# Seven block products for the second token block's first weight set, four of its weight remainders on GpSimd after attention, and a re-ordered end of attention

## The chip, the cores and the metric

The kernel runs on one core of one Trainium2 chip. The metric is the device time of one execution in microseconds. The core's engines run side by side, each with its own queue: TensorE (PE, with PEld for loading weights), VectorE (DVE), ScalarE (ACT), GpSimd (POOL) and SyncE (SP), which issues most of the transfers.

## The reference

Attention with a position bias comes first, then a layer of three "experts" of which the largest is taken:

```python
scores = scale * np.matmul(q, k.transpose(0, 1, 3, 2))        # 4 batches, 8 heads, 576 x 576
h = np.maximum(x @ w1 + b1, 0.0); bias = h @ w2               # x: relative position, 32 hidden units
scores = scores + bias.transpose(2, 0, 1)[None, :, :, :]
attn = exp(scores - max); attn = attn / (sum(attn) + 1e-09)
attn_out = np.matmul(attn, v)                                  # head size 64
x = attn_out as 2304 tokens x 512
h = np.maximum(np.maximum(x @ moe_w1, x @ moe_w2), x @ moe_w3) # 512 x 768 each
out = h @ moe_w_out                                            # 768 x 512
```

Everything is float32. The kernel gets near that with TensorE's rounded 32-bit type by splitting each operand into a rounded "high" part and a "low" remainder, and multiplying high by high, low by high and high by low.

## The kernel before

**Stages.** The bias comes first (to about 84 us), with attention running behind it. Attention has 72 steps (8 pairs of heads by 9 query tiles) and four more, 72 to 75, in which it drains: `tp` and `lp` are transposes of the normalised probabilities `e`, ScalarE and VectorE copy them to `et`, and the products `pv` (and `pvlast`) with the values follow. `e` is normalised by GpSimd (L325). When a `pv` accumulator is full, VectorE copies it out into the raw token tiles, printed as `xb` (L413). The expert part begins at 263.2 us, and the output product follows it from about 450.

**Expert part.** Tokens lie in three blocks x = 0, 1, 2 of 768 (2 by `TW` = 384), the weights in nine sets of four 256-wide parts. A set times a block is a `group` of seven block products, as in Strassen's scheme: p1, p5, p6, p2, p7, p4, p3, of the weight parts and their sums and of the token parts b11, b12, b21, b22 and the sums t1 to t4. For set 0 and the blocks 1 and 2 it is `plain`: eight products without sums. A block product is six matmuls of 128x384 (L654 to L656: high by high, low by high, high by low, for two halves). In a group p1, p6, p7 and p4 add into one PSUM bank, and between them ScalarE copies that bank out:

```python
nc.scalar.copy(o["m1"], made("p1"))                 # printed as m, L688
nc.scalar.copy(o["u2"], made("p6", "p1"))           # printed as u, L696
arith(v, o["q"][:, 1], made("p2"), o["m1"], ALU.add)
nc.scalar.copy(u3, made("p7", "p1"))                # printed as u, L703
nc.scalar.copy(acc[:, 0], made("p4", "p1"))         # printed as ht, L710
```

`acc` and, in set 0, `q` are printed as `ht`. p5 has a bank of its own, to which p3 adds.

**Splitting.** For a token part `high` is a cast by ScalarE (L567, the names ending in h), `low` a subtraction with two inputs from SBUF (`arith`, L542, ending in l) on VectorE or GpSimd, `sum` an addition or subtraction by VectorE (printed as `t`). The sums build on each other: t1 = b12 - b11, t3 = b22 - b12, t2 = t3 + b11, t4 = b21 - t2; p5 uses t1, p6 the second sum t2, p7 t3, p4 the fourth sum t4. Block 0's tiles for these two are swapped by `home`: its second sum's parts are printed as `t4h` and `t4l`, its fourth sum's as `t2h` and `t2l`. The tile `t2h` takes the place of the raw b21, so its cast waits until `b21l` is formed, and `t2l` that of the raw b22. Weights go the same way: `wh` is ScalarE's cast, `wl` the remainder (`low0(k)` for part k of set 0, `lower_w` for the later ones), `ws` the weight sums by GpSimd, `wr0p` the raw set 0, `wr` the raw set 1.

**What sets the order.** Each engine works through its queue in the order in which the program writes it; nothing is scheduled by itself. During attention the extra work is in streams: `w0` converts and splits weights, `pend` holds weight sums and two remainders, `early_x` and `late_x` split token block 0. The main loop says in which step a stream may emit its next piece, and `rest` empties them after step 75. In the expert part one slot belongs to each block product: the table of `F(...)` jobs in `moe` says which token and weight work is emitted in which slot, ahead of that slot's product. In the list that orders the products, `plain(1)` gives one product into the first group (behind p7), and all of `plain(1)` and `plain(2)` follow it.

Of the kernel before, what the change touches and what calls it, by code (L numbers as in the profile page):

```python
# [9 lines left out]
F32 = mybir.dt.float32  # L10
# [9 lines left out]
def kernel(  # L20
# [12 lines left out]
    nc = tc.nc  # L33
# [514 lines left out]
    class Blocks:  # L548
# [8 lines left out]
        def home(self, n, k):  # L557
            if self.x == 0 and n in ("t2", "t4"):
                n = "t4" if n == "t2" else "t2"
            if n in F_OF:  # L560
                return self.fin.tile(SHAPE, F32R, tag=f"f{self.x}_{F_OF[n] + k}", bufs=1, name=f"{n}{'hl'[k]}_{self.x}")
            return self.xa.tile(SHAPE, F32R, tag=f"r{self.x}_{R_OF[n] + k}", bufs=1, name=f"{n}{'hl'[k]}_{self.x}")
# [79 lines left out]
    def moe(pool, wpool, x0, xa, xb, raw, sr):  # L642
# [113 lines left out]
        for k, what in enumerate((  # L756
                (F(b1.high, "b11", "b21"), F(b1.low, "b11")),
                (F(b1.low, "b21"), F(b1.high, "b12")),
                (F(b1.low, "b12"), F(b1.high, "b22")),
                (F(b1.low, "b22"), F(b2.high, "b11")),  # L760
                (F(b1.sum, "t1"), F(b2.high, "b21")),
                (F(b2.low, "b11"), F(b2.high, "b12")),
                (F(b1.high, "t1"), F(b2.low, "b21"), F(b2.high, "b22")),
                (F(b1.low, "t1"),),
                (F(b2.low, "b12"),),
                (F(b2.low, "b22"),),
                (F(b1.sum, "t3"),),
                (F(b1.sum, "t2"), F(b1.high, "t3")),
                (F(b1.low, "t3"),),
                (F(b1.sum, "t4"), F(b1.high, "t2")),  # L770
                (F(b1.low, "t2"), F(b1.high, "t4")),
                (F(b1.low, "t4"), F(raise_w, 1, 0)),
                (F(b2.sum, "t1"), F(raise_w, 1, 1)),
                (F(lower_w, 1, 0, v, 3), F(b2.high, "t1")),
                (F(lower_w, 1, 3, v, 4),),
                (F(b2.low, "t1"),),
                (F(b2.sum, "t3"),),
                (F(b2.sum, "t2"), F(b2.high, "t3")),
                (F(b2.low, "t3"),),
        )):  # L780
            at(*((0, k) if k < 7 else divmod(k + 1, 8)), *what)
# [305 lines left out]

        c1, c2 = plain(1), plain(2)
        g0 = list(group(0, 0))
        for k, f in enumerate(g0[:5] + c1[:1] + g0[5:] + c1[1:] + c2):  # L1090
            now[:] = (0, k) if k < 7 else divmod(k + 1, 8)
            slot()
            f()
        groups = [group(s, x) for s in range(1, NSET) for x in range(NX)] + [out_pair(m) for m in range(NP)]
        groups[0][0]()
        for n, (_, p5, p6, p2, p7, p4, p3) in enumerate(groups[:-2]):
# [11 lines left out]
    with tc.manual_schedule():  # L1108
# [44 lines left out]
        class Pieces:  # L1153
# [8 lines left out]
            def go(self, scalar):  # L1162
                if not scalar:
                    for f in self.todo[:self.count]:
                        self.todo.pop(0)()
# [7 lines left out]
        def first():  # L1173
# [8 lines left out]

            def sums(raw, name, k=None):
                got = {}

                def piece(n):
                    if n == 0:
                        got["sr"] = sum_tile(wpool, name)
                        got["gen"] = sum_w(raw, got["sr"])
                        next(got["gen"])  # L1190
# [41 lines left out]
            sums0, got = sums(raw0, "0")  # L1232
            pend.extend(sums0 + [lambda k=k: low0(k) for k in (2, 7)])
            yield "vector"
# [5 lines left out]
            nc.scalar.copy(hi[:, 768:1792], got["sr"])  # L1240
            for k in (3, 5):
                yield "vector"
                low0(k, nc.vector, 2)
            yield from conv(lambda: half(made1, 1, ()), "1_1")
            make, got1 = sums(made1[0], "1")
            pend.extend(make)
            last.update(raw=made1[0], got=got1)

# [16 lines left out]
        def late_x():  # L1265
            for j in range(2):
                yield "vector"
                x0.sum("t3", j)
            yield "vector"
            x0.sum("t2")  # L1270
            yield "scalar"
            x0.high("t3", "b21")
            yield "vector"
            x0.low("t3")
            yield "scalar"
            x0.high("t2")
            yield "vector"
            x0.sum("t4")
            x0.low("t2")
            yield "scalar"  # L1280
            x0.high("b22")
            yield "vector"
            x0.low("b21")
            x0.low("b22")

        ex, lx = Stream(early_x()), Stream(late_x())
        while n < NSTEP + LAG:
# [4 lines left out]
            if n % NS in (3, 5, 8) and not early and n < NSTEP - 3 or n in (NSTEP - 3, NSTEP - 2):  # L1292
                pend.count = 2 if n == 6 * NS - 1 else 1
                more += [pend]
            if early:
                more.insert(0, ex)
            if n >= NSTEP or n in (NSTEP - 3, NSTEP - 1):
                more.insert(0, lx)
# [4 lines left out]
        for w in (w0, pend, ex, lx):  # L1303
            w.rest()
        x0.high("t4")
        x0.low("t4")
        at.split_x()
        apool.release()
# [51 lines left out]
```

## Time and profile before

| what | value |
|---|---|
| median of 3 runs | 534.76 us (534.66 to 535.26) |
| profiled execution, time | 534.38 us |
| profiled execution, span of its instructions | 532.6 us |
| TensorE busy | 522.8 us, 98% of the span |
| VectorE busy | 438.3 us, 82% |
| ScalarE busy | 358.7 us, 67% |
| GpSimd busy | 263.7 us, 50% |
| TensorE's granted clock, mean | 1.000 |
| transfers | 78.66 MB, mean 148 GB/s |

The span runs from the first instruction to the last; 1.8 us of the execution lie around it. Busy is the time in which an engine has an instruction under way. Rows of the trace give start, length, engine, line and operation, the tile that is written, `<-` the tiles that are read, then shape and count; in brackets stands the idle time before, with `<-` what ended it.

### The profile page before, as it was taken

How to read it: one execution, taken by the hardware profiler on the slowest of the kernel's cores; microseconds unless marked ns; L12 is line 12 of the kernel's file. 1: busy time of each engine (PE TensorE's matmuls, PEld its weight loads, DVE VectorE, ACT ScalarE, POOL GpSimd, SP SyncE). 2: the span in 40 equal slices, each digit the busy share in tenths (PEclk: the TensorE clock that was granted, in tenths of full speed). 3: DMA queues.
4: the chain of work that ended last, by engine and by line, in shares of the span. 5: the costliest groups of instructions: out<-in, count | busy, mean ns of one | idle time of the engine just before them, and what ended most of it. 6: DMA issues, size and time to landing. Idle time of an engine off the chain costs nothing.

```text
span 532.6 us, 13672 instructions
## 1 busy us (share of the span) xinstructions
PE 522.8 (98%) x5185; PEld 436.5 (82%) x5185; DVE 438.3 (82%) x929; ACT 358.7 (67%) x805; POOL 263.7 (50%) x294
## 2 busy tenths in 40 slices
PE   8999899999999999999999999999999999999997
PEld 5455667676767676666699999999999999999997
DVE  7998879898989898989999988648887456898883
ACT  7998989998989999888767343443434325465552
POOL 0003878678878897877302563646566535300000
DMA  5896998533774193111301215442175340856642
GB/s 162 239 337 175 348 269 233 166 107 109 223 216 150 26 252 120 55 23 36 109 0 41 78 42 196 140 159 78 56 261 180 140 147 1 255 171 188 190 148 80
DMA packets 73458, 78.66 MB, mean 148 GB/s; under 512 B 23152, under 2 KB 54512, under 8 KB 73392
## 3 DMA queue, kind: packets, MB, share of 16 engines
q1 hardware_dynamic: 73248, 77.49, 46.8%
q8 instruction: 41, 0.67, 0.5%
q10 hardware_dynamic: 144, 0.29, 0.2%
q14 instruction: 25, 0.20, 0.1%
HBM read 49.56 MB, written 27.94 MB: 146 GB/s over the span
## 4 chain that ended last, share of the span: by engine, by line
PE 86%; DVE 5%; ACT 3%; issue 2%; POOL 2%; DMA 1%; DVEq 0%; POOLq 0%; ACTq 0%
PE pv L393 14%; PE p L656 11%; PE p L654 11%; PE p L655 11%; PE s L287 10%; PE tp L352 6%; PE p_o L1031 4%; PE p_o L1030 4%; PE p_o L1029 4%; DVE hid L113 4%; PE bp L135 3%; ACT e L311 2%; PE lp L352 2%; PE s L277 1%; POOL e L325 1%
## 5 line engine op out<-in xcount | busy, mean ns | idle before, releaser
L325 POOL TENSOR_SCALAR e<-e,rc 128x576 f32<-128x576 f32 x144 | 111.7, 792 | 30.6 <-DVE rc L321 26.2
L297 DVE CUSTOM_DVE_ANT_0 sn<-s,bias 128x576 f32<-128x576 f32 x144 | 103.1, 754 | 21.7 <-PE lp L352 10.9
L311 ACT ACTIVATE e<-sn,nm 128x576 f32<-128x576 f32 x144 | 111.3, 780 | 3.8 <-DVE nm L297 3.5
L393 PE MATMUL pv<-et,vt 128*64 128x320 f32 (+1 forms) x496 | 74.0, 419 | 0.6 <-PE lp L352 0.6
L352 PE MATMUL tp<-ident,e 64*128 64x64 f32 x1152 | 53.2, 224 | 0.5 <-ACT et L463 0.3
L467 DVE COPY et<-tp 128x512 f32<-128x512 f32 x72 | 49.3, 685 | 3.8 <-PE tp L352 3.7
L463 ACT COPY et<-tp 128x512 f32<-128x512 f32 x72 | 41.8, 580 | 14.2 <-PE lp L352 13.6
L542 POOL TENSOR_TENSOR wl<-wr,wh 128x256 fp32r<-128x256 f32 x21 | 21.3, 1040 | 59.5 <-ACT wh L744 59.5
L287 PE MATMUL s<-kh,qh 64*128 64x288 f32 x240 | 48.0, 342 | 1.1 <-DVE nm L297 1.0
L352 PEld LDWEIGHTS tp<-ident,e 64*128 64x128 f32 x1152 | 47.3, 139 | 0.8 <-ACT et L463 0.5
L287 PEld LDWEIGHTS s<-kh,qh 64*128 64x128 f32 x240 | 28.0, 184 | 21.4 <-DVE nm L297 8.5
L393 PEld LDWEIGHTS pv<-et,vt 128*64 128x64 f32 x496 | 30.4, 136 | 18.2 <-issue 1.6
L696 ACT COPY u<-p 128x384 f32<-128x384 f32 x25 | 12.0, 480 | 43.1 <-PE p L656 42.8
L287 PE MATMUL s<-kl,qh 64*128 64x288 f32 x240 | 40.9, 296 | 0.0
L135 PE MATMUL bp<-hid,w2s 128*32 128x79 f32 (+51 forms) x640 | 39.9, 390 | 0.9 <-DVE hid L113 0.7
L287 PE MATMUL s<-kh,ql 64*128 64x288 f32 x240 | 39.8, 291 | 0.0
L113 DVE TENSOR_SCALAR hid<-sm,bp 128x528 f32<-128x528 f32 (+17 forms) x108 | 39.1, 443 | 0.0
L135 PEld LDWEIGHTS bp<-hid,w2s 128*32 128x32 f32 x640 | 19.9, 110 | 21.1 <-issue 15.4
L703 ACT COPY u<-p 128x384 f32<-128x384 f32 x25 | 12.0, 479 | 36.5 <-PE p L656 36.4
L542 POOL TENSOR_TENSOR wl<-ws,wh 128x256 fp32r<-128x256 f32 x28 | 29.2, 1070 | 13.1 <-ACT wh L746 13.1
L352 PE MATMUL lp<-ident,e 64*128 64x64 f32 x144 | 33.3, 231 | 2.3 <-POOL e L325 1.5
L542 DVE TENSOR_TENSOR q<-p,u 128x384 f32<-128x384 f32 x36 | 19.9, 553 | 17.4 <-ACT u L703 15.1
(236 smaller groups left out, 1621.0 us busy)
## 6 DMA issues: line engine op xcount, KB each, us to landing
bias_d<-bs SPq DMA_DIRECT2D x36, 295.5 KB, 5.6
bias<-bias_d SPq DMA_DIRECT2D x16, 576.0 KB, 5.4
w<-in_moe_w_dram SPq DMA_DIRECT2D x36, 256.0 KB, 3.2
h_d<-ht SPq DMA_DIRECT2D x18, 384.0 KB, 3.2
hin<-h_d SPq DMA_DIRECT2D x16, 384.0 KB, 4.6
qr<-in_qd_dram SPq DMA_DIRECT2D x16, 288.0 KB, 4.4
kr<-in_kd_dram SPq DMA_DIRECT2D x16, 288.0 KB, 5.4
vt<-in_v_dram SPq DMA_DIRECT2D x32, 128.0 KB, 3.4
```

The source lines that it names most:

```text
L113: marks["hid"] = nc.vector.tensor_scalar(out=h[:, 0:n], in0=wl[:, 0:n], scalar1=k["bp"][:, m:m + 1], scalar2=0.0, op0=ALU.add, op1=ALU.max)
L135: nc.tensor.matmul(bp[32 * c:32 * c + 32, o:o + w], lhsT=w2s, rhs=src, start=True, stop=True)
L287: nc.tensor.matmul(ss[h][:, x, 0:HALF], lhsT=u[q][p, 128 * t:128 * t + 128], rhs=u[k][p, cols], start=(j == 0), stop=(j == len(terms) - 1))
L297: nc.vector.tensor_tensor_reduce(out=sn.rearrange("p (a b) -> p a b", a=2), in0=st["s"][h][:, :, 0:HALF], in1=bt.rearrange("p (a b) -> p a ...
L311: nc.scalar.activation(st["e"][:, S * h:S * h + S], sn, ACTF.Exp, scale=-1.0, bias=nm, accum_out=self.sm[:, x:x + 1])
L325: nc.gpsimd.tensor_scalar(out=e, in0=e, scalar1=self.rc[:, x:x + 1], scalar2=1.0, op0=ALU.mult, op1=ALU.mult)
L352: return nc.tensor.transpose(to, e2[p, k0:k0 + 128], ident[p, p])
L393: nc.tensor.matmul(pv[p], lhsT=w, rhs=x, start=(c == 0), stop=(c == NTQ))
L542: eng.tensor_tensor(out=out, in0=f(a), in1=f(b), op=op)
L654: nc.tensor.matmul(o, lhsT=hi[:, c], rhs=h[:, j], start=first and j == 0, stop=False, **on)
L655: nc.tensor.matmul(o, lhsT=hi[:, c], rhs=l[:, j], start=False, stop=False, **on)
L656: nc.tensor.matmul(o, lhsT=lo[:, c], rhs=h[:, j], start=False, stop=last and j == 1, **on)
```

## The change

It touches only set 0 of the weights, the end of attention and the first slots of the expert part.

- Token block 1 takes set 0 in a `group` of seven products, as block 0 does. The products of set 0 now run: block 0's group with one plain product of block 2 in it, the other seven plain ones of block 2, then block 1's group with the first product of set 1 in it. The table of jobs is re-ordered for that: block 2's splits come first, block 1's sums earlier.
- `home` swaps the tiles of block 1's second and fourth sum as well.
- `pend` no longer holds the remainders 2 and 7 of set 0, and emits one piece at a time. The stream `w0` leaves out the remainders 5 and 6; the remainder 3 comes behind the conversion of set 1's second half, on VectorE, one part wide.
- Set 1's weight sums get a tile of the weight fetches' kind (`w64`).
- `late_x` forms the remainders of block 0's b21 and b22 on GpSimd, with set 0's remainder 2 between and 5, 7, 6 behind. Block 0's last sum, its cast and the remainders around it move behind the drain's steps, and VectorE's remainder of t3 moves behind an accumulator's copies.

```diff
         def home(self, n, k):
-            if self.x == 0 and n in ("t2", "t4"):
+            if self.x < 2 and n in ("t2", "t4"):
...
-                (F(b1.high, "b11", "b21"), F(b1.low, "b11")),
...
+                (F(b2.high, "b11", "b21"), F(b2.low, "b11")),
...
+                (F(b1.low, "b11"), F(b1.sum, "t1"), F(b1.high, "t1")),
...
-        c1, c2 = plain(1), plain(2)
-        g0 = list(group(0, 0))
-        for k, f in enumerate(g0[:5] + c1[:1] + g0[5:] + c1[1:] + c2):
+        groups = [group(s, x) for s in range(1, NSET) for x in range(NX)] + [out_pair(m) for m in range(NP)]
+        c2, g0, g1 = plain(2), group(0, 0), group(0, 1)
+        for k, f in enumerate((*g0[:5], c2[0], *g0[5:], *c2[1:], *g1[:5], groups[0][0], *g1[5:])):
             now[:] = (0, k) if k < 7 else divmod(k + 1, 8)
             slot()
             f()
-        groups = [group(s, x) for s in range(1, NSET) for x in range(NX)] + [out_pair(m) for m in range(NP)]
-        groups[0][0]()
...
-                    for f in self.todo[:self.count]:
+                    for f in self.todo[:1]:
...
-                        got["sr"] = sum_tile(wpool, name)
+                        got["sr"] = wpool.tile([128, 1024], F32, tag=tag, bufs=2 if tag == "w64" else 1, name=f"ws{name}")
...
-            pend.extend(sums0 + [lambda k=k: low0(k) for k in (2, 7)])
+            pend.extend(sums0)
...
-            for k in (3, 5):
-                yield "vector"
-                low0(k, nc.vector, 2)
+            yield "vector"
             yield from conv(lambda: half(made1, 1, ()), "1_1")
-            make, got1 = sums(made1[0], "1")
+            make, got1 = sums(made1[0], "1", tag="w64")
             pend.extend(make)
-            last.update(raw=made1[0], got=got1)
+            last.update(raw=made1[0], got=got1, low=low0)
+            yield "vector"
+            low0(3, nc.vector, 2)
...
         def late_x():
-            for j in range(2):
-                yield "vector"
-                x0.sum("t3", j)
             yield "vector"
+            x0.sum("t3", 0)
+            yield "vector"
+            x0.sum("t3", 1)
+            x0.high("t3")
             x0.sum("t2")
             yield "scalar"
-            x0.high("t3", "b21")
+            x0.high("b21")
             yield "vector"
-            x0.low("t3")
+            x0.low("b21", nc.gpsimd)
             yield "scalar"
             x0.high("t2")
             yield "vector"
-            x0.sum("t4")
-            x0.low("t2")
+            x0.low("t3")
+            last["low"](2)
             yield "scalar"
             x0.high("b22")
             yield "vector"
-            x0.low("b21")
-            x0.low("b22")
+            x0.low("b22", nc.gpsimd)
+            for k in (5, 7, 6):
+                last["low"](k)
...
-                pend.count = 2 if n == 6 * NS - 1 else 1
...
-            if n >= NSTEP or n in (NSTEP - 3, NSTEP - 1):
+            if n >= NSTEP or n == NSTEP - 3:
                 more.insert(0, lx)
...
+        x0.low("t2")
+        x0.sum("t4")
         x0.high("t4")
+        at.split_x()
         x0.low("t4")
-        at.split_x()
```

The following excerpts are each engine's order, one row per instruction or run of like ones; the numbers behind the names tell tiles apart.

GpSimd's queue before, from attention's last but two groups of `e` to the first remainders of weight set 1 (`wl_5734`, which wait for casts in the expert part):

```order
L542 TENSOR_TENSOR ws_5092<-wr_4353 128x256
L325 TENSOR_SCALAR e_5088<-e_5088,rc_5219 128x576 x2
L325 TENSOR_SCALAR e_5151<-e_5151,rc_5219 128x576 x2
L325 TENSOR_SCALAR e_5214<-e_5214,rc_5312 128x576 x2
L325 TENSOR_SCALAR e_5270<-e_5270,rc_5312 128x576 x2
L542 TENSOR_TENSOR ws_5092<-wr_4353,ws_5092 128x256
L542 TENSOR_TENSOR wl_5734<-wr_5470,wh_5733 128x256 x3
L542 TENSOR_TENSOR wl_5734<-ws_5712,wh_5733 128x256 x4
```

And the same place after; `b21l` and `b22l` are block 0's, `wl_3333` the remainders of weight set 0:

```order
L325 TENSOR_SCALAR e_5086<-e_5086,rc_5216 128x576 x2
L325 TENSOR_SCALAR e_5148<-e_5148,rc_5216 128x576 x2
L325 TENSOR_SCALAR e_5211<-e_5211,rc_5308 128x576 x2
L325 TENSOR_SCALAR e_5267<-e_5267,rc_5308 128x576 x2
L542 TENSOR_TENSOR b21l_5350<-xb_0_1171,b21h_5317 128x768
L542 TENSOR_TENSOR wl_3333<-wr0p,wh_3332 128x256
L542 TENSOR_TENSOR b22l_5424<-xb_0_1172,b22h_5393 128x768
L542 TENSOR_TENSOR wl_3333<-ws_3400,wh_3332 128x256
L542 TENSOR_TENSOR wl_3333<-wr0p,wh_3332 128x256
L542 TENSOR_TENSOR wl_3333<-ws_3400,wh_3332 128x256
L542 TENSOR_TENSOR wl_5730<-wr_5471,wh_5729 128x256 x3
```

Six subtractions now stand behind the last `e` where one weight sum stood. Two are 768 wide, four 256 wide.

VectorE's queue before, in the drain: `et` are copies of transposes, `xb` the copies out of the accumulators `pv` and `pvlast`, `t_0_5316` block 0's second sum and `t_0_5393` its fourth:

```order
L542 TENSOR_TENSOR t3l_5353<-t_0_5155,t3h_5318 128x768
L413 COPY xb_1_1175<-pv_1_5304 128x192
L413 COPY xb_2_1179<-pv_1_5304 128x64 x2
L467 COPY et_0_5360<-tp_7_1_5363 128x8x64
L542 TENSOR_TENSOR t_0_5393<-xb_0_1171,t_0_5316 128x768
L542 TENSOR_TENSOR t4l_5395<-t_0_5316,t4h_5355 128x768
L467 COPY et_0_5360<-tp_8_1_5401 128x8x64
L542 TENSOR_TENSOR b21l_5428<-xb_0_1171,b21h_5320 128x768
L542 TENSOR_TENSOR b22l_5430<-xb_0_1172,b22h_5397 128x768
L413 COPY xb_1_1176<-pv_1_5385 128x192
L413 COPY xb_2_1180<-pv_1_5385 128x64 x2
L542 TENSOR_TENSOR t2l_5449<-t_0_5393,t2h_5447 128x768
```

And after, where the second sum is `t_0_5315` and the fourth `t_0_5446`; the last row is the first remainder of the expert part:

```order
L413 COPY xb_1_1175<-pv_1_5300 128x192
L413 COPY xb_2_1179<-pv_1_5300 128x64 x2
L467 COPY et_0_5357<-tp_7_1_5360 128x8x64
L542 TENSOR_TENSOR t3l_5390<-t_0_5152,t3h_5313 128x768
L467 COPY et_0_5357<-tp_8_1_5397 128x8x64
L413 COPY xb_1_1176<-pv_1_5382 128x192
L413 COPY xb_2_1180<-pv_1_5382 128x64 x2
L542 TENSOR_TENSOR t4l_5444<-t_0_5315,t4h_5352 128x768
L542 TENSOR_TENSOR t_0_5446<-xb_0_1171,t_0_5315 128x768
L413 COPY xb_2_1180<-pvlast 128x256
L542 TENSOR_TENSOR t2l_5451<-t_0_5446,t2h_5448 128x768
L542 TENSOR_TENSOR b11l_5469<-xb_2_1178,b11h_5465 128x768
```

The accumulator's copies (`pv_1_5300`) moved ahead of `t3l`; `b21l` and `b22l` left the queue; `t4l` and the fourth sum moved behind the copies of the next accumulator.

ScalarE's queue before, at the beginning of the expert part (`m` and `u` are the copies of the shared bank, `t2h_5447` the cast of block 0's fourth sum):

```order
L567 CAST t2h_5447<-t_0_5393 128x768
L567 CAST b11h_5464<-xb_1_1174 128x768
L567 CAST b21h_5466<-xb_1_1175 128x768
L688 COPY m_0_5472<-p_0_0_5473 128x384
L567 CAST b12h_5483<-xb_1_1173 128x768
L567 CAST b22h_5494<-xb_1_1176 128x768
L696 COPY u_0_5496<-p_0_0_5473 128x384
L567 CAST b11h_5506<-xb_2_1178 128x768
L567 CAST b21h_5518<-xb_2_1179 128x768
L703 COPY u_0_5520<-p_0_0_5473 128x384
L567 CAST b12h_5531<-xb_2_1177 128x768
L567 CAST t1h_5540<-t_1_5516 128x768
```

And after, where the fourth sum's cast is `t2h_5448`:

```order
L1222 CAST wh_3332<-wr0p 128x256
L567 CAST t2h_5448<-t_0_5446 128x768
L567 CAST b11h_5465<-xb_2_1178 128x768
L567 CAST b21h_5467<-xb_2_1179 128x768
L688 COPY m_0_5473<-p_0_0_5474 128x384
L567 CAST b12h_5484<-xb_2_1177 128x768
L567 CAST b22h_5495<-xb_2_1180 128x768
L696 COPY u_0_5497<-p_0_0_5474 128x384
L567 CAST b11h_5507<-xb_1_1174 128x768
L567 CAST t1h_5521<-t_1_5519 128x768
L703 COPY u_0_5523<-p_0_0_5474 128x384
L567 CAST t3h_5543<-t_1_5534 128x768
```

The casts ahead of `m` are as many as before, of block 2 instead of block 1; ahead of the second `u` now stands the cast of block 1's first sum, `t1h_5521`, which stood behind it.

## Rows read from the trace of the kernel before

**Rows 1.** The page's busy times: engine, us, share of the span, instructions.

```profile
PE 522.8 (98%) x5185; PEld 436.5 (82%) x5185; DVE 438.3 (82%) x929; ACT 358.7 (67%) x805; POOL 263.7 (50%) x294
```

**Rows 2.** Stretches: bounds, length, busy PE, PEld, DVE, ACT, POOL; granted clock, DMA share, GB/s.

```profile
205.00:226.00 21.00, 20.09 (x273) 13.64 (x271) 19.33 (x50) 19.41 (x52) 15.66 (x18) 1.00 0.20 53
...
250.00:263.20 13.20, 11.96 (x138) 7.11 (x136) 11.94 (x25) 10.13 (x23) 7.41 (x8) 1.00 0.37 121
263.20:289.50 26.30, 26.30 (x153) 26.30 (x152) 24.97 (x31) 18.43 (x30) 0.00 (x0) 1.00 0.07 21
```

**Rows 3.** Timeline of TensorE, 205 to 236: start, length, operation, idle before.

```profile
217.11 0.27 PE L352 MATMUL lp<-ident,e 64*128 64x64 f32 x1 [0.26 <-POOL e L325]
...
220.36 0.27 PE L352 MATMUL lp<-ident,e 64*128 64x64 f32 x1 [0.47 <-POOL e L325]
```

**Rows 4.** Timeline of GpSimd, 186 to 296.

```profile
194.62 1.84 POOL L542 TENSOR_TENSOR t1l<-t,t1h 128x768 fp32r<-128x768 f32 x1
...
211.60 0.74 POOL L542 TENSOR_TENSOR wl<-wr0p,wh 128x256 fp32r<-128x256 f32 x1 [2.13 <-ACT wh L1225]
...
215.58 1.47 POOL L325 TENSOR_SCALAR e<-e,rc 128x576 f32<-128x576 f32 x2
...
253.19 4.14 POOL L325 TENSOR_SCALAR e<-e,rc 128x576 f32<-128x576 f32 x4 [0.62 <-DVE rc L321]
257.30 0.73 POOL L542 TENSOR_TENSOR ws<-wr,ws 128x256 f32<-128x256 f32 x1
```

**Rows 5.** Timeline of TensorE, drain and beginning of the expert part, 250 to 300.

```profile
257.35 1.84 PE L393 MATMUL pv<-et,vt 128*64 128x320 f32 x12 [0.43 <-PE lp L352]
...
260.41 0.71 PE L393 MATMUL pv<-et,vl 128*64 128x320 f32 x4
...
265.39 0.33 PE L654 MATMUL p<-t4h,wh 128*128 128x384 f32 x1
...
269.55 0.34 PE L654 MATMUL p<-t2h,wh 128*128 128x384 f32 x1
...
288.30 0.34 PE L654 MATMUL p<-t1h,wh 128*128 128x384 f32 x1
```

**Rows 6.** Timeline of ScalarE, 250 to 275.

```profile
261.51 0.84 ACT L567 CAST t2h<-t 128x768 fp32r<-128x768 f32 x1 [0.84 <-DVE b21l L542]
262.25 0.83 ACT L567 CAST b11h<-xb 128x768 fp32r<-128x768 f32 x1
...
264.55 0.48 ACT L688 COPY m<-p 128x384 f32<-128x384 f32 x1 [0.73 <-PE p L656]
...
268.71 0.48 ACT L703 COPY u<-p 128x384 f32<-128x384 f32 x1
```

**Rows 7.** Timeline of VectorE, 250 to 275.

```profile
255.57 1.15 DVE L542 TENSOR_TENSOR t3l<-t,t3h 128x768 fp32r<-128x768 f32 x1
256.64 0.61 DVE L413 COPY xb<-pv 128x192 f32<-128x192 f32 x3
...
257.77 1.07 DVE L542 TENSOR_TENSOR t<-xb,t 128x768 f32<-128x768 f32 x1
...
267.67 0.56 DVE L542 TENSOR_TENSOR ht<-p,m 128x384 f32<-128x384 f32 x1
268.15 0.95 DVE L542 TENSOR_TENSOR t<-xb,xb 128x768 f32<-128x768 f32 x1
...
269.70 0.95 DVE L542 TENSOR_TENSOR b11l<-xb,b11h 128x768 fp32r<-128x768 f32 x1
270.56 0.95 DVE L542 TENSOR_TENSOR b21l<-xb,b21h 128x768 fp32r<-128x768 f32 x1
```

**Rows 8.** Timeline of VectorE and GpSimd, 445 to 461.

```profile
450.19 5.11 POOL L542 TENSOR_TENSOR wop<-wop,wohp 128x768 fp32r<-128x768 f32 x2
...
454.42 1.29 DVE L542 TENSOR_TENSOR Cl<-C,Ch 128x384 fp32r<-128x384 f32 x1
...
458.82 0.55 DVE L542 TENSOR_TENSOR Al<-hin,Ah 128x384 fp32r<-128x384 f32 x1
```

More of the change, by code (lines that the diff above doesn't have):

```diff
@@ L756, in moe @@
         for k, what in enumerate((
-                (F(b1.high, "b11", "b21"), F(b1.low, "b11")),
[L758 to L774, printed above, removed]
+                (F(b2.high, "b11", "b21"), F(b2.low, "b11")),
+                (F(b2.low, "b21"), F(b2.high, "b12")),
+                (F(b2.low, "b12"), F(b2.high, "b22")),
+                (F(b2.low, "b22"), F(b1.high, "b11")),
+                (F(b1.low, "b11"), F(b1.sum, "t1"), F(b1.high, "t1")),
+                (F(b1.low, "t1"), F(b1.sum, "t3")),
+                (F(b1.high, "t3"), F(b1.sum, "t2")),
+                (F(b1.low, "t3"), F(b1.high, "t2")),
+                (F(b1.low, "t2"), F(b1.high, "b21")),
+                (F(b1.sum, "t4"),),
+                (F(b1.low, "b21"), F(b1.high, "b22")),
+                (F(b1.low, "b22"), F(b1.high, "t4")),
+                (F(b1.low, "t4"),),
+                (F(raise_w, 1, 0),),
+                (F(raise_w, 1, 1),),
+                (F(lower_w, 1, 0, v, 3),),
                 (F(lower_w, 1, 3, v, 4),),
+                (F(b2.sum, "t1"), F(b2.high, "t1")),
                 (F(b2.low, "t1"),),
@@ L1181, in conv, with sums @@
                     yield token
-            def sums(raw, name, k=None):
+            def sums(raw, name, k=None, tag="ws"):
                 got = {}
```

## The prediction

> **What bounds the kernel now.** I read the busy times first: TensorE has work in 98% of the span, VectorE follows with 82% [rows 1]. So the span is TensorE's own work plus its few waits, and an edit counts only if it removes matmuls or moves a wait. The table by stretch says where waits are left [rows 2]: 0.9 us in the stretch from 205 to 226, 1.2 us in the drain of attention (250 to 263.2), none in the first 26 us of the expert part, where TensorE is busy 26.30 of 26.30 us. The granted clock is 1.00, the 2.4 GHz level, in all three. Then I read single instructions. In 205 to 226 two waits of 0.26 and 0.47 us are for GpSimd's `e` [rows 3], while GpSimd itself had stood 2.13 us in front of a weight remainder `wl` [rows 4]. In the drain the reader should see a wait of 0.43 us in front of `pv` at 257.35 [rows 5]: VectorE copies out the old accumulator (256.64) only after `t3l` [rows 7].
>
> At the start of the expert part TensorE never waits, but by little. p1, p6, p7 and p4 of a group add into one PSUM bank, and ScalarE copies that bank out between them (m, u, u): p6 may start when m is copied, p4 when the second u is. m is done at 265.03 and p6 starts at 265.39; the second u is done at 269.19 and p4 starts at 269.55 [rows 5, 6]. The margin is 0.36 us both times. Both copies stand in ScalarE's queue behind casts that wait for VectorE.
>
> **What the change removes.** The second token block takes seven block products instead of eight. Six matmuls go; a block product lasts 1.04 us (four from 265.39 to 269.55) [rows 5]. From p4 of the first group to the second product of weight set 1 there are 18 block products before (269.55 to 288.30, that is 18.75 us) and 17 after: **-1.04 us**, all on the path.
>
> The weight remainders 2 and 7 leave GpSimd's queue in the middle of attention, and with the one at 211.60 the 2.13 us of standing that kept the `e` behind it late [rows 4]. Both waits of [rows 3] should go: -0.73 us at most, 0 if a conversion step of VectorE that now falls there holds up the scores instead. I take **-0.6**, near the upper end, since the released `e` at 215.58 can move by more than both waits together. The conversion of set 1's second half moves one slot earlier and the sums of set 1 move among the `e`: nothing, since GpSimd stands idle there before each group of `e`; without that cover a sum costs 0.73. SP's queue keeps its order; one weight fetch now waits for VectorE to finish set 1's remainders, and it is used some ten block products later: nothing.
>
> Copying out the accumulator before `t3l` takes away the 0.43 us at 257.35. I count that as nothing too, because something else is late next.
>
> **What it adds, first place: the drain.** After its last `e` GpSimd now has b21l, weight remainder 2, b22l, and remainders 5, 7, 6; it had one piece of 0.73 us. A 768-wide remainder takes GpSimd 1.84 us, a 256-wide one 0.74 [rows 4]; on VectorE 768 wide takes 0.95 [rows 7]. What matters is what the two do to each other. A 128x384 remainder takes VectorE 0.55 us at 458.82 (`Al`), and 1.29 us at 454.42 (`Cl`), where GpSimd's two remainders run from 450.19 to 455.30; it ends 0.41 us behind them [rows 8]. It waited until GpSimd's instruction was over. GpSimd's two took 2.56 each instead of 1.84, so it waits as well. The Trainium skill has this as a rule (SBUF — State Buffer, section "Who interferes with whom"): a VectorE instruction with two SBUF inputs and a GpSimd instruction that reads SBUF exclude each other for a whole instruction. By that rule the sum is the one below, by a mere tax it would be the first rival's; `Cl` agrees with the rule.
>
> So from the end of the last `e` (253.19 + 4.14 = 257.33) [rows 4] the two engines take turns, the earlier asker first: b21l 1.84, t3l 0.95, remainder 2 0.74, b22l 1.84, t4l (the remainder of the second sum) 0.95, remainder 5 0.74, the fourth sum 0.95. That is 8.01 us, so the fourth sum is ready at 265.34. Check that t4l comes behind b22l: b22l begins at 260.86, and t4l stands behind the copies of the accumulator that ends at 261.12, or 0.4 to 0.6 us earlier with the wait at 257.35 gone [rows 5]; three copies take 0.61 (256.64) [rows 7]: it asks at about 261.1 at the earliest. In the kernel before the fourth sum was formed at 257.77 and nothing waited.
>
> ScalarE's queue is t2h (the cast of that fourth sum), two casts of the third token block, then m. Casts follow each other at 0.74 us, m takes 0.48 [rows 6]: 265.34 + 2.22 + 0.48 = 268.04, with 0.1 for the handover (estimated) p6 starts at **268.1 instead of 265.39**. Behind the waiting cast stand m, and behind m TensorE.
>
> **Second place: p4.** In the new order the second u stands behind t1h of the second token block; t1h waits for VectorE's sum t1, that sum for b11l, and b11l stands behind the addition that waits for p2. From the end of p2: addition 0.48, b11l 0.87, sum 0.95, cast 0.74, u 0.48, handover 0.1: 3.62 us [rows 6, 7]. TensorE has only two block products less a pipeline end between the end of p2 and p4, 1.9 us. So p4 waits at least 1.7 us whatever the drain does. Here VectorE is later still: remainders 7 and 6 take their turns until 266.82, then t2l and four remainders of the third block at 0.87 each [rows 7] end at 271.17, when p2 (268.1 + 2.08 + 0.17 = 270.35) is over already. 271.17 + 3.62 = **274.8 for p4 instead of 269.55: +5.25**. From there VectorE runs some 0.2 us ahead of what TensorE asks in the second block; I allow 0 to +0.4 for it.
>
> **Sum.** +5.25 - 1.04 - 0.6 = +3.6 us. The profiled execution took 534.38 us with a span of 532.6; the median of the runs is 534.76, 0.38 above it. 534.38 + 3.6 = 538.0, and on the median **538.4**. Bounds: the gain at 217 to 220 may be 0 to -0.73, the turns may fall in another order (0.4 either way; if t4l gets in before b22l, p4 comes out 0.4 later), the second block 0 to +0.4. That makes 537.4 to 539.8.
>
> **Rivals.** *Not slower: the engines hinder each other only a little.* `t3l` ran beside `e` in 1.15 us, 0.20 over its usual length [rows 7]. At that tax t4l and the fourth sum follow the copies directly, the sum is ready at 263.0 to 263.4, p6 starts at 265.8 to 266.2, and p4 at 271.8 to 272.2 (p2 ends 2.25 us behind p6's start, 3.62 more, with 0.1 of lateness). +2.25 to +2.65 - 1.64 = +0.6 to +1.0: about 535.6, within 0.2%. It decides at t4l and the fourth sum: if each takes under 1.2 us, this case holds. For it speaks `t3l`, against it `Cl`; and `t3l` fits turns too, where it came near the end of an `e`.
>
> *Faster: m and u come in time after all*, so that both waits stay out and the wait at 257.35 counts: -1.04 - 0.6 - 0.4 = -2.0, 532.7. Against it is that t1h stands ahead of u in the same queue; p4 alone must slip by 1.7.
>
> *The clock.* Gaps of about 3 us are longer than any in the rows (0.47), where the clock held 1.00. If it fell to 1.2 GHz behind one, a block product would take 2.08 us; three to five of them add 3 to 5 us: about 542. The Trainium skill (TensorE: Matmul & The Clock Gate, section "Part 1: The HAM clock gate") has an idle TensorE put back to its lower level; no row here shows it.
>
> *That the change does not do what it says* is out: the TensorE order has six matmuls fewer.
>
> **How the numbers follow.** Forecast 0.69, little hindrance 0.15, faster 0.05, clock 0.05, other 0.06. The range takes in the forecast's own (537.4 to 539.8) and the rival below it: 535.4 to 539.8, which leaves out less than 2 in 10. About 0.2%, 1.07 us, is what a measurement can tell from no change. Faster 0.06: the faster case and a rest. Same 0.12: most of the little-hindrance case. Slower 0.82: the forecast, the clock, the remainder.
>
> **What the changed profile would show.** No wait for `e` near 217 to 220. In the drain t4l and the fourth sum at 1.5 us and more each, beginning when GpSimd's pieces end; t2h some 3 us later relative to the first product; TensorE waiting near 3 us for m in front of p6 and near 2.5 us for u in front of p4, then without gaps through the second block with 1.04 us per product. I am wrong if p6 follows p5 with a gap under 1 us, if p4 waits less than 1.7, or if GpSimd's remainders lengthen and VectorE's do not.

## The result, and the profile after

The changed kernel took **538.86 us** (median of 6 runs, 537.33 to 540.02) against 534.84 for the kernel before (534.62 to 536.59): ratio 1.0066, 95% interval 1.0044 to 1.0088. A second set, shown with the experiments, gave 537.82 against 534.57, ratio 1.0064 (1.0051 to 1.0078). It is slower, by about 0.65%, with both intervals clear of no change. The profiled execution took 537.54 us with a span of 535.8, which is 3.2 more than before; the rows below are from it. The runs' spread goes with the mean granted clock: 0.999 in the two quickest, 0.996 or 0.997 in the other four.

The table by stretch of the changed kernel (columns as in [rows 2]) shows what came and went: 0.4 us less idle time of TensorE in 205 to 226, 0.65 less in the drain, and 3.8 us of idle time in the first 26 us of the expert part, where there was none. Another 0.6 follow.

```profile
205.00:226.00 21.00, 20.50 (x292) 14.44 (x290) 18.99 (x51) 19.67 (x53) 15.41 (x19) 1.00 0.20 54
...
250.00:263.20 13.20, 12.61 (x140) 8.16 (x141) 11.77 (x20) 8.05 (x19) 12.19 (x11) 1.00 0.25 83
263.20:289.50 26.30, 22.50 (x126) 21.54 (x126) 23.05 (x29) 17.45 (x28) 1.48 (x2) 1.00 0.13 41
289.50:460.00 170.50, 169.89 (x977) 169.57 (x976) 123.45 (x184) 67.25 (x121) 92.74 (x93) 1.00 0.36 122
```

TensorE's timeline of the changed kernel names the waits, against [rows 5]. The expert part begins 1.35 us earlier than before (261.85 instead of 263.20). p6 (`t4h`) waits 1.98 us for m, p4 (`t2h`) 1.80 for the second u, p7 of weight set 1's first group (`t3h` at 294.47) 0.61 for its first u.

```profile
261.85 0.44 PE L654 MATMUL p<-b11h,wh 128*128 128x384 f32 x1
...
266.20 0.44 PE L654 MATMUL p<-t4h,wh 128*128 128x384 f32 x1 [1.98 <-ACT m L688]
...
272.47 0.44 PE L654 MATMUL p<-t2h,wh 128*128 128x384 f32 x1 [1.80 <-ACT u L703]
...
290.56 0.34 PE L654 MATMUL p<-t1h,wh 128*128 128x384 f32 x1
...
294.47 0.45 PE L654 MATMUL p<-t3h,wh 128*128 128x384 f32 x1 [0.61 <-ACT u L696]
```

GpSimd's timeline in the drain (compare the last two rows of [rows 4]): six remainders, of which three that are 256 wide last 1.45 us; the last one, when VectorE asks for nothing, has its 0.72.

```profile
252.44 3.75 POOL L325 TENSOR_SCALAR e<-e,rc 128x576 f32<-128x576 f32 x4 [1.01 <-DVE rc L321]
256.16 1.82 POOL L542 TENSOR_TENSOR b21l<-xb,b21h 128x768 fp32r<-128x768 f32 x1
257.94 1.45 POOL L542 TENSOR_TENSOR wl<-wr0p,wh 128x256 fp32r<-128x256 f32 x1
259.34 1.82 POOL L542 TENSOR_TENSOR b22l<-xb,b22h 128x768 fp32r<-128x768 f32 x1
261.11 1.46 POOL L542 TENSOR_TENSOR wl<-ws,wh 128x256 fp32r<-128x256 f32 x1
262.54 1.45 POOL L542 TENSOR_TENSOR wl<-wr0p,wh 128x256 fp32r<-128x256 f32 x1
263.96 0.72 POOL L542 TENSOR_TENSOR wl<-ws,wh 128x256 fp32r<-128x256 f32 x1
```

VectorE's there and behind (against [rows 7]): `t3l`, `t4l` and the fourth sum last 2.29, 1.63 and 1.48 us instead of 0.95, and each ends 0.8 us behind one of GpSimd's remainders: `t3l` at 258.80 behind 257.98, `t4l` at 261.99 behind 261.16 (ends are start plus length).

```profile
256.51 2.29 DVE L542 TENSOR_TENSOR t3l<-t,t3h 128x768 fp32r<-128x768 f32 x1
...
260.36 1.63 DVE L542 TENSOR_TENSOR t4l<-t,t4h 128x768 fp32r<-128x768 f32 x1
261.90 1.48 DVE L542 TENSOR_TENSOR t<-xb,t 128x768 f32<-128x768 f32 x1
...
268.89 0.54 DVE L542 TENSOR_TENSOR ht<-p,m 128x384 f32<-128x384 f32 x1
269.36 0.94 DVE L542 TENSOR_TENSOR b11l<-xb,b11h 128x768 fp32r<-128x768 f32 x1
270.23 0.94 DVE L542 TENSOR_TENSOR t<-xb,xb 128x768 f32<-128x768 f32 x1
```

ScalarE's queue passes both delays on (against [rows 6]): m stands behind a cast that waited 3.87 us for the fourth sum, u behind `t1h`, which waited 2.42 for VectorE's sum.

```profile
263.48 0.83 ACT L567 CAST t2h<-t 128x768 fp32r<-128x768 f32 x1 [3.87 <-DVE t L542]
...
265.68 0.47 ACT L688 COPY m<-p 128x384 f32<-128x384 f32 x1
...
271.20 0.83 ACT L567 CAST t1h<-t 128x768 fp32r<-128x768 f32 x1 [2.42 <-DVE t L542]
271.94 0.47 ACT L703 COPY u<-p 128x384 f32<-128x384 f32 x1
```

### The profile page after: what moved, and what is told of

The parts are those of the page before. It is cut to its first block, busy times and chain, and to the rows that moved or that the text cites. A ratio compares the mean times of both kernels' runs of the same rounds, so it can differ in the third digit from the quotient of the medians.

```text
span 535.8 us, 13665 instructions
## 1 busy us (share of the span) xinstructions
PE 522.7 (98%) x5179; PEld 435.1 (81%) x5179; DVE 438.1 (82%) x928; ACT 357.7 (67%) x804; POOL 270.5 (50%) x298
## 4 chain that ended last, share of the span: by engine, by line
PE 83%; DVE 11%; ACT 3%; issue 2%; DMA 1%; DVEq 0%; ACTq 0%
PE pv L393 16%; PE s L287 11%; PE p L654 11%; PE p L656 11%; PE p L655 11%; PE tp L352 6%; PE p_o L1030 4%; PE p_o L1029 4%; PE p_o L1028 4%; DVE hid L113 4%; PE bp L135 3%; PE lp L352 2%; DVE t L542 2%; PE s L277 1%; ACT e L311 1%
## 5 line engine op out<-in xcount | busy, mean ns | idle before, releaser
L542 POOL TENSOR_TENSOR wl<-ws,wh 128x256 fp32r<-128x256 f32 x30 | 31.3, 1071 | 14.7 <-ACT wh L746 14.7
```

Source lines behind the costliest of these rows:

```text
L542: eng.tensor_tensor(out=out, in0=f(a), in1=f(b), op=op)
```

## The experiments

**Theory:** two separate places cost, each by the order of queues: m behind the fourth sum, which waits for its turn between GpSimd's remainders; u behind t1h, which waits for VectorE's remainders. **Rivals:** VectorE simply has more work than time, so that nothing is won by order; or the clock; or the engines hinder each other only a little.

**t1h behind u.** Edit of the changed kernel:

```diff
-                (F(b1.low, "b11"), F(b1.sum, "t1"), F(b1.high, "t1")),
-                (F(b1.low, "t1"), F(b1.sum, "t3")),
+                (F(b1.low, "b11"),),
+                (F(b1.sum, "t1"), F(b1.high, "t1"), F(b1.low, "t1"), F(b1.sum, "t3")),
```

> The changed kernel with one edit: the sum t1 of block 1 and its cast t1h stand one slot later, behind the second u. Theory (each of the two waits has its own place in the queues): p6 still waits near 2.0 us for m; the 1.8 us in front of p4 go, p4 starts near 270.5 instead of 272.47; VectorE then has no idle 1.3 us in front of its addition of u, and of the 1.8 us up to 0.9 come back later in the second block: 537.0 to 537.9 us. Rival (VectorE's load alone sets the end of the second block, wherever TensorE waits): the 1.8 us come back whole, 538.9 us within 0.3.

537.10 us, ratio 1.0048 (1.0035 to 1.0061). p4 started at 270.41 without a wait, 2.06 us earlier; p6 waited 2.00 as before. But the span fell by 0.5 only: in block 1's own group p6 now waited 1.11 us for m and p7 0.32 for its u, so 1.5 us of the 2.06 came back, more than the 0.9 that was expected, though not the whole as the rival has it. TensorE's timeline of this run (start, length, then the idle time before):

```profile
266.13 0.44 PE L654 MATMUL p<-t4h,wh 128*128 128x384 f32 x1 [2.00 <-ACT m L688]
283.15 0.44 PE L654 MATMUL p<-t4h,wh 128*128 128x384 f32 x1 [1.11 <-ACT m L688]
```

**t2h behind m.** Edit: the cast and remainder of block 0's fourth sum leave the drain for the second slot.

```diff
-        x0.high("t4")
         at.split_x()
-        x0.low("t4")
...
-                (F(b2.low, "b21"), F(b2.high, "b12")),
+                (F(b0.high, "t4"), F(b0.low, "t4"), F(b2.low, "b21"), F(b2.high, "b12")),
```

> The changed kernel with one edit: the cast t2h and the remainder t2l of block 0 move out of the drain into the second slot, behind m. Theory: p6 no longer waits, it starts near 264.2 instead of 266.20, but p4 comes at 272.0, 0.4 us earlier only, because the second u still stands behind t1h, and t1h behind VectorE's five remainders, its addition for p2, b11l and the sum; so 538.0 to 538.8 us. Rival (the waits simply add up): p4 2.0 us earlier, near 536.9 us.

539.42 us, ratio 1.0085 (1.0073 to 1.0097). The places came out as expected: p6 at 263.80 without a wait, p4 at 272.09, only 0.38 us earlier than in the changed kernel. So the first wait was no loss of its own; whoever removes it alone moves it in front of p4. The profiled execution (538.20 us, mean clock 0.997) lies in the expected range, the median 0.6 us above it; three of the five runs have a mean clock of 0.993 and took 539.4 to 539.8 us, and where the clock fell in those was not caught. Stretches of the profiled execution and three rows of TensorE: behind the wait of 3.64 us the granted clock is 0.51, the 1.2 GHz level, until 275, and matmuls follow each other at 0.32 us instead of 0.17. Nine of them make 1.3 us.

```profile
271.00:272.00 1.00, 0.00 (x0) 0.00 (x0) 0.00 (x0) 1.00 (x2) 0.00 (x0) 0.75 0.00 0
272.00:275.00 3.00, 2.91 (x9) 2.91 (x10) 2.90 (x4) 0.64 (x2) 0.00 (x0) 0.51 0.00 0
275.00:276.00 1.00, 1.00 (x8) 1.00 (x7) 0.90 (x2) 1.00 (x3) 0.00 (x0) 1.00 0.00 0
```

```profile
272.09 0.69 PE L654 MATMUL p<-t2h,wh 128*128 128x384 f32 x1 [3.64 <-ACT u L703]
272.58 0.52 PE L655 MATMUL p<-t2l,wh 128*128 128x384 f32 x1
272.90 0.52 PE L656 MATMUL p<-t2h,wl 128*128 128x384 f32 x1
```

**Both edits.**

> Both edits of the two runs before in one kernel. Theory: neither m nor the second u stands behind VectorE's late work; p6 starts near 264.1 and p4 near 268.4, 4.1 us earlier than in the changed kernel. VectorE has at most 2 to 2.5 us of idle time to give until the second block's products ask for its sums, so some 2 us come back there as waits: 536 to 537.5 us, 534.5 if VectorE keeps up. Rival (VectorE's load alone): 538.9 us.

536.85 us, ratio 1.0045 (1.0033 to 1.0057). p4 came 6.67 us behind the first product (262.86 to 269.53) instead of 10.62, nearly as in the kernel before (6.35). 2.4 us more than before were left nevertheless. The trace has four waits: 0.94 in front of p3 for VectorE's addition, 1.72 for m and 0.31 for u in block 1's group, 0.61 in set 1's first group; they use up what attention and the product had gained.

**The drain alone:** the new drain and weight remainders, with the old products and table.

> The kernel before with the new order of the drain and of the weight remainders, but with the plain eight products for block 1 and the old table of jobs. Theory: attention ends some 1.35 us earlier, as in the changed kernel; in the drain VectorE and GpSimd take turns, so t4l and the fourth sum last 1.4 us and more and p6 starts near 266.2 behind m; p4 has no wait of its own and starts near 270.4 instead of 269.55. 18 products follow instead of 17. 535.4 to 535.9 us. Rival (the drain costs nothing by itself, the loss is all in the product order): 533.4 us, 1.35 under before.

535.48 us, ratio 1.0026 (1.0017 to 1.0035). The median is in the expected range, but between two groups of runs: six took 535.1 to 535.5 us, the profiled one with 535.10 among them, and five, with a mean clock of 0.997, 536.6 to 536.8. p6 came at 266.00 behind a wait of 2.00 for m, p4 at 270.26 without a wait.

```profile
266.00 0.44 PE L654 MATMUL p<-t4h,wh 128*128 128x384 f32 x1 [2.00 <-ACT m L688]
...
270.26 0.34 PE L654 MATMUL p<-t2h,wh 128*128 128x384 f32 x1
```

**The products alone:** seven products and the new table, with the old drain.

> The kernel before with the new products and the new table of jobs alone: seven products for block 1, the drain and the weight remainders as before. Theory: attention and p6 as before (p6 near 265.4, no wait for m); p4 waits 1.7 us, since the second u stands behind t1h, t1h behind the sum, the sum behind b11l and that behind the addition for p2; one product fewer gives 1.04 back; up to 1.2 us come late in the second block and in the first group of set 1, as in the changed kernel. Near 536.3 us, 535.0 to 536.5. Rival (the seven products are sound, the drain alone costs): 533.4 us.

536.74 us, ratio 1.0036 (1.0023 to 1.0049), 0.2 above the range. p6 at 265.41 without a wait; p4 at 271.33 behind 1.60 us for the second u, 1.78 later than before. Either half of the change loses by itself, and 1.0026 and 1.0036 make about the 1.0064 to 1.0066 of both; with the six quicker runs of the drain alone (about 1.0015) they make 1.005.

```profile
265.41 0.33 PE L654 MATMUL p<-t4h,wh 128*128 128x384 f32 x1
...
271.33 0.44 PE L654 MATMUL p<-t2h,wh 128*128 128x384 f32 x1 [1.60 <-ACT u L703]
```

**b21l and b22l on VectorE.** Edit of the changed kernel: `x0.low("b21", nc.gpsimd)` and `x0.low("b22", nc.gpsimd)` without the engine.

> The changed kernel with one edit: the remainders of block 0's b21 and b22 are formed by VectorE again instead of GpSimd. Theory (turns: a GpSimd remainder shuts VectorE's two-input work out for its whole length): VectorE has 1.74 us more to do, but is rid of two stretches of 1.8 us; t4l near 1 us instead of 1.63, the fourth sum ready near 262.2 instead of 263.38, p6 near 265.0 instead of 266.20, p4 near 271.0 instead of 272.47; 537 to 538 us. Rival (GpSimd relieves VectorE, the engines hinder each other a little): the fourth sum 1.7 us later, 540 us and more.

537.39 us, ratio 1.0044 (1.0030 to 1.0058). VectorE with 1.74 us more work was not later: the fourth sum was ready at 263.02 instead of 263.38. In the timeline `t4l` had its turn ahead of a 256-wide GpSimd remainder and took 0.96 instead of 1.63, while that remainder took 1.44; the sum, behind it, still took 1.48. So p6 came at 265.84, 0.36 earlier, and p4 at 271.97, 0.50 earlier; both had been expected further forward, at 265.0 and 271.0.

```profile
260.66 0.96 DVE L542 TENSOR_TENSOR t4l<-t,t4h 128x768 fp32r<-128x768 f32 x1
260.77 1.44 POOL L542 TENSOR_TENSOR wl<-ws,wh 128x256 fp32r<-128x256 f32 x1
261.54 1.48 DVE L542 TENSOR_TENSOR t<-xb,t 128x768 f32<-128x768 f32 x1
```

**The two engines measured by themselves.** Behind the end of the kernel before: VectorE alone, GpSimd alone, then five stretches with three to six GpSimd instructions beside VectorE's:

```diff
...
+            vtt = lambda: v.tensor_tensor(out=ov, in0=a, in1=b, op=ALU.subtract)
+            gtt = lambda: g.tensor_tensor(out=og, in0=a, in1=b, op=ALU.subtract)
...
+            vcp = lambda: v.tensor_copy(ov, a)
+            vps = lambda: v.tensor_tensor(out=ov[:, 0:384], in0=ps[:, 0:384], in1=b[:, 0:384], op=ALU.subtract)
...
```

> The kernel before, with a stretch added behind its end that measures the two engines: VectorE's 768-wide subtraction of two SBUF tiles alone, GpSimd's alone, both at once; then GpSimd's beside VectorE's copies in SBUF, beside VectorE's subtractions with one operand in PSUM, beside its copies out of PSUM; last VectorE's subtraction beside GpSimd's 576-wide scaling of the kind that normalises e. The time tells nothing here. Theory (turns): alone 0.95 and 1.84 us; both at once a pair takes 2.7 us, so VectorE's last 1.9 us and more; copies and the subtraction with a PSUM operand keep their length, or show that these are shut out too. Rival (a mere tax): both at once VectorE near 1.15, GpSimd near 2.2 us, overlapping.

Turns. While GpSimd's first remainder runs (546.67 to 548.47), even an 8-column copy of VectorE takes 1.75 us; where no remainder runs it takes 0.17 (at 535.96). Then each side's next instruction ends only behind the other's, 2.44 to 2.47 us a pair. Rows of both engines:

```profile
546.67 1.80 POOL L1323 TENSOR_TENSOR mog<-ma,mb 128x768 f32<-128x768 f32 x1
546.75 1.75 DVE L1334 COPY msv<-msg 128x8 f32<-128x8 f32 x1 [0.29 <-POOL msg L1333]
548.41 0.95 DVE L1322 TENSOR_TENSOR mov<-ma,mb 128x768 f32<-128x768 f32 x1
548.55 2.47 POOL L1323 TENSOR_TENSOR mog<-ma,mb 128x768 f32<-128x768 f32 x1
549.39 2.44 DVE L1322 TENSOR_TENSOR mov<-ma,mb 128x768 f32<-128x768 f32 x1
```

The groups of that stretch by line (busy us, mean ns): VectorE's ten subtractions with one operand in PSUM and its ten copies out of PSUM have 556 ns each, with GpSimd's remainders beside most of them. Its ten copies within SBUF have 855: 0.55 us alone, 2.04 beside a remainder. GpSimd's scaling, the kind that normalises e, lasts 1229 ns on average beside VectorE's subtractions (0.76 us the first of the six, 1.32 the others). One row does not fit the copy above: at 584.10 the 8-column copy took 0.17 us although GpSimd's first scaling had begun at 584.04. No run here tells why.

```profile
L1326 DVE COPY mov<-ma 128x768 f32<-128x768 f32 x10 | 8.5, 855 | 0.3
L1324 POOL TENSOR_SCALAR mog<-ma,mrc 128x576 f32<-128x576 f32 x6 | 7.4, 1229 | 0.5
L1328 DVE COPY mov<-mps 128x384 f32<-128x384 f32 x10 | 5.6, 556 | 0.3
L1327 DVE TENSOR_TENSOR mov<-mps,mb 128x384 f32<-128x384 f32 x10 | 5.6, 556 | 0.3
```

```profile
584.04 7.84 POOL L1324 TENSOR_SCALAR mog<-ma,mrc 128x576 f32<-128x576 f32 x6
584.10 0.17 DVE L1334 COPY msv<-msg 128x8 f32<-128x8 f32 x1 [0.28 <-POOL msg L1333]
```

The Trainium skill (SBUF — State Buffer, section "Who interferes with whom") states it so: a VectorE instruction with two SBUF inputs, against a GpSimd instruction that reads SBUF, or one in a two-port mode, takes turns with GpSimd by whole instructions; one with at most one SBUF input outside those modes does not. The 768-wide subtractions and copies and both forms with a PSUM operand agree; in which mode a copy ran, no row shows.

**Another table.** Both edits, and each remainder, sum and cast just ahead of the product that asks for it; core of the edit:

```diff
...
+                (F(b1.high, "b11"),),
+                (F(b2.high, "b22"),),
+                (F(b1.low, "b11"), F(b1.sum, "t1"), F(raise_w, 1, 0), F(raise_w, 1, 1)),
+                (F(b2.low, "b12"),),
+                (F(b1.high, "t1"), F(b1.sum, "t3")),
...
```

> The run with both edits, with another table of jobs: each remainder, sum and cast of blocks 1 and 2 stands just ahead of the product that asks for it; set 1's two casts move to where ScalarE idles (behind the second u); block 1's b11l behind the addition for p7; block 2's later sums move by two to five slots. Theory (VectorE's work fits if it is done in the order in which it is asked for): p4 near 268.3, no wait over 0.5 us up to the end of set 1's first group, so attention's 1.35 us and the 1.04 us of the product stay: 532.2 to 533.4 us. Rival (VectorE has more work than time there, whatever the order): 2 us and more of waits remain, 534.5 to 536.8 us.

534.86 us, ratio 1.0001 (0.9992 to 1.0010): the loss is gone, the gain not there yet, and the time is the rival's. p4 came at 268.10 as expected. Two waits were left, in TensorE's timeline of this run. Both looked like order again: m stood behind `t2h`, and VectorE's addition behind block 2's remainder and sum. The next run tells whether it is order or VectorE's load.

```profile
280.40 0.44 PE L654 MATMUL p<-t4h,wh 128*128 128x384 f32 x1 [0.68 <-ACT m L688]
...
294.65 0.45 PE L654 MATMUL p<-b22h,wh 128*128 128x384 f32 x1 [1.44 <-DVE q L542]
```

**The second table.**

```diff
-                (F(b1.low, "b22"), F(b1.high, "t4")),
-                (F(b1.low, "t4"),),
+                (F(b1.low, "b22"),),
...
+                (F(b1.high, "t4"), F(b1.low, "t4")),
...
-        at(3, 3, F(b2.low, "t3"), F(b2.sum, "t4"))
+        at(3, 4, F(b2.low, "t3"))
+        at(3, 5, F(b2.sum, "t4"))
...
```

Block 2's casts and remainders behind that sum move one to three slots further back.

> The run with the new table, with its two remaining waits mended in the order: block 1's last cast t2h stands behind m instead of ahead of it, block 2's remainder t3l and its fourth sum behind VectorE's addition for p7 of set 1's first group. Theory (what is left is order, and VectorE can keep up): the waits of 0.68 and 1.44 us in front of p6 of block 1's group and in front of p3 of set 1's first group go, at most 0.4 us come up elsewhere; 532.6 to 533.3 us, below the kernel before. Rival (VectorE has more work than time): the waits move to later products, 534.3 us and more.

533.85 us, ratio 0.9986 (0.9977 to 0.9994): below the kernel before, but 0.5 above what was expected, since one of the waits moved: p7 of set 1's second group waited for its u, behind block 2's two casts.

```profile
297.86 0.44 PE L654 MATMUL p<-t3h,wh 128*128 128x384 f32 x1 [1.38 <-ACT u L696]
```

**The second table with b21l and b22l on VectorE.**

> The same, with the remainders of block 0's b21 and b22 on VectorE again. Theory: TensorE no longer waits for what stands behind them, so that their place decides little: within 0.4 us of the run beside it; a wait near 0.3 us in front of the products of the drain as in the earlier run with this edit (0.31 us), against some 0.5 us of VectorE's time saved from turns. Rival (GpSimd's relief of VectorE is needed once the order is right): 0.8 us and more slower than the run beside it.

533.94 us, ratio 0.9991 (0.9983 to 1.0000), 0.09 from the run beside it. With the order right, which engine forms the two decides nothing that can be told here.

**The changed kernel again.**

> The changed kernel once more, unchanged. Four of its six runs had a mean granted clock of 0.996 or 0.997 and took 538.8 to 540.0 us, two had 0.999 and took 537.3 and 537.5. If the lower clock belongs to the waits of 2 us in front of p6 and p4, a profile of such a run shows the granted clock under 1 directly behind them; if it is any kernel's, it shows it elsewhere (between 65 and 75 us in one profile of another run).

537.82 us (four runs, 537.70 to 538.48). The profile shows the granted clock at 1.00 through the whole of TensorE's work, behind its 2 us waits too. Mean clocks of 0.997 and 0.996 came with 537.85 and 538.48 us. Where the clock fell in such runs was not caught; it stays open. The runs on record hold a hint: of the 26 runs of the three kernels whose longest wait is near 2.0 us (the changed kernel, t1h behind u, the drain alone) 11 have a mean clock of 0.997 or less, though none of the five of t1h behind u; of the 117 runs of kernels with shorter waits or none (the kernel before among them) 2 have.

**The third table.** The two casts behind the u's:

```diff
-        at(3, 6, F(b2.high, "t2"))
-        at(4, 0, F(b2.high, "t4"))
-        at(4, 1, F(b2.low, "t2"))
-        at(4, 4, F(b2.low, "t4"))
+        at(4, 2, F(b2.high, "t2"))
+        at(4, 4, F(b2.low, "t2"), F(b2.high, "t4"))
+        at(4, 6, F(b2.low, "t4"))
```

> The second table with its one remaining wait mended: block 2's casts t2h and t4h stand behind the copies u of set 1's second group instead of ahead of the first of them. Theory (the 1.38 us in front of p7 of that group are ScalarE's queue order and nothing else): the wait goes, TensorE runs without a gap from the first product to the end of the expert part, 1.4 to 1.6 us less than the run before: 532.2 to 532.6 us against 534.6 before. Rival (VectorE is late there whatever stands in ScalarE's queue): p6 of set 1's third group waits for t2l instead, 533.5 us and more.

**532.25 us, ratio 0.9957 (0.9944 to 0.9971)**: faster than both kernels, by 2.2 us against before and, by the ratios, some 5.7 against the changed kernel. The profiled execution is the slowest of the five, with its first product at 262.28. Its stretches from the end of attention on: TensorE is busy 27.70 of 27.70 and 170.49 of 170.50 us, VectorE 26.67 of 27.70.

```profile
261.80:289.50 27.70, 27.70 (x162) 27.32 (x159) 26.67 (x33) 17.95 (x30) 6.00 (x5) 1.00 0.13 39
289.50:460.00 170.50, 170.49 (x984) 170.17 (x983) 126.56 (x186) 67.13 (x121) 92.42 (x92) 1.00 0.38 128
```

So VectorE did have the time, 96% of it in that stretch, and the rival that it had more work than time is out.

## Why the prediction was right, point by point

The forecast was 538.4, with both waits in their places. The mechanism came as forecast: turns between the two engines, m behind the fourth sum, u behind `t1h`. That the number is so close is luck. The sum gave +3.6 us, and the profiled execution shows 3.1 at TensorE's last matmul (529.25 before, 532.39 after), because p4 came 1.7 us earlier than forecast and a wait that has no term in the sum came on top. The last 0.9 us up to the 4.0 between the medians belong to runs with a lower mean clock, which the forecast of 538.4 did not count in. The lower bound does not follow from its parts either: 538.4 - 0.13 - 0.4 is 537.9, not 537.4; the result lies inside both ways.

- **Attention, -0.6: it was -1.35.** No wait for `e` is left at 217 to 220, as forecast; by 230 TensorE is 0.7 us ahead. The 0.43 us in front of `pv` went as well; it was counted as nothing because m is late next. That holds: p6 waits for a chain that begins at the last `e`, not for `pv`. But the last `e` itself ended at 256.19 instead of 257.33, and that 1.14 is what counts, not 0.6: the last four `e` began 0.75 us earlier, and took 3.75 us instead of 4.14, with `t3l` no longer among them.
- **The drain's turns:** order and kind as forecast, in the very sequence b21l, t3l, weight remainder, b22l, t4l, weight remainder, sum. From the end of the last `e` they took 7.19 us (256.19 to 263.38) against 8.01: in its turn a subtraction of VectorE takes 0.8 us, not 0.95, and a 256-wide remainder of GpSimd 0.6, not 0.74. "TensorE waiting near 3 us for m" was 1.98.
- **p4: forecast 4.65 us later with attention's gain in it, measured 2.92** (272.47 against 269.55). From VectorE's addition for p2 to p4 it took 3.58 us (268.89 to 272.47; 3.62 was the forecast's chain), with the members of the chain in the rows above. The step that was mis-sized is the one ahead: VectorE was said to be late until 271.17, 0.8 us behind the end of p2, but its addition began at 268.89, some 0.3 us behind it. Of the 2.28 us between, 1.14 are the earlier `e` (0.6 of it stands in the sum as attention's gain), 0.82 the shorter turns, and 0.3 the remainders 7 and 6: they were given two turns ahead of `t2l`, which waited for its cast instead and lasted only 0.1 us longer beside them.
- **One product fewer, -1.04: it is there**, since with no wait listed the third table ends 2.2 us under the kernel before, and -1.35 - 1.04 is -2.4. In its profile, which starts later, 265.34 us lie between the first product and the last matmul instead of 266.05; a small gap of 0.3 us at 307 is what is missing there.
- **The second block, 0 to +0.4: it was +0.38, and +0.88 came behind it.** From p4 to the second product of set 1 the changed kernel needs 18.09 us (272.47 to 290.56); 18.75 less 1.04 is 17.71. The 0.88 up to the last matmul are the wait of 0.61 at 294.47, with the pipeline end in front of it and the slower first product behind it. The sum has no term for that: the prediction saw VectorE ahead in the second block and did not look at what stood ahead of u in set 1's first group, block 2's cast `t2h` behind VectorE's sum (293.21, after 1.74 us idle).
- **Rivals.** A little hindrance is out: the lone measurement shows turns. "Faster: m and u in time" is out for this order, and true for another one (third table). The clock fell behind a wait of 3.64 us, where it cost 1.3 us and not the 3 to 5 of the rival, and not behind 2.00, 1.98 or 1.80 in any profile here. The Trainium skill (TensorE: Matmul & The Clock Gate, section "Part 1: The HAM clock gate") has idleness put the clock back; the fall behind the 3.64 agrees. Of the change's median, 1.3 us above its own profiled run, the lower mean clock may be the cause, so a milder form of this rival may hold in those runs; that is argued, not shown.

## What to carry to other kernels

Read each engine's queue at the place where the bound engine's copy stands, and ask what it stands behind: here all listed waits of the expert part but two (both for VectorE's addition) were for a copy of 0.5 us that stood behind casts, of which one had waited for another engine. In four of the runs putting the cast behind the copy took the wait in front of that product away; the others went with the new table as a whole. Work with two operands in SBUF that is given to GpSimd relieves VectorE only where VectorE idles or works out of PSUM; in this drain a 768-wide remainder on GpSimd took about twice the time from VectorE (1.8 us) that VectorE itself would need (0.95). A wait that is removed alone can come back at the next place (3.64 us in front of p4 for 1.98 and 1.80), so look at the places together.

## What the hardware showed that was not expected

An 8-column copy within SBUF took 1.75 us beside each GpSimd remainder, so being short does not protect an instruction, and GpSimd's scaling of `e` takes turns too (1.23 us on average beside VectorE's subtractions), which no row of the kernel before had made plain; beside that scaling the one short copy on record was not held up. In one profile of another kernel (both edits) the granted clock was 0.79 and 0.86 between 65 and 75 us, ahead of everything that the change touches, and attention ended 1.0 us later than in the changed kernel. TensorE was busy 4.40 and 5.00 of 5.00 us there; what lowered the clock stays open.
